# Two attention blocks and two Fourier blocks on one core: 384 and 128 column blocks share a PSUM bank, and one layer norm gets another gate

## The chip, the cores and the metric

The kernel runs on one core of a Trainium2 chip. A core has TensorE (PE, matrix products, with its weight loads as PEld), VectorE (DVE), ScalarE (ACT), GpSimd (POOL) and SyncE (SP, which here issues every DMA), each with its own instruction queue worked in order. They share SBUF, and TensorE writes to eight PSUM banks of 128 partitions x 512 fp32 columns. The metric is the device time of one execution in microseconds (us), the median of several runs.

## The reference

A sequence x of 2048 rows by 512 columns goes through four blocks, A, B, A, B, each with a layer norm in front and a residual around it:

```
x = x + A(layernorm(x)); x = x + B(layernorm(x)); and both again

A: 32 heads of width 16, four segments of 512 rows, for each segment s:
   p     = softmax(q k^T / 4 + causal mask);  a_dot = p v
   a_mem = phi(q) M / (phi(q) z + 1e-6)       phi(t) = t+1 if t > 0 else exp(t)
   o     = g a_mem + (1 - g) a_dot            g = sigmoid(beta) per head
   M += phi(k)^T v;  z += sum phi(k)
   result o @ wo
B: real part of a DFT over rows and columns:  Cr (x Dr^T) - Ci (x Di^T)
```

The mask is causal in the segment, so of the 4 x 4 blocks of 128 x 128 of each head only ten count. The DFT matrices are inputs.

## The kernel before

Products are made from fp16 halves: a value is scaled and split into a high and a low half, and three matmuls (high x high, high x low, low x high) stand for one. Two blocks A+B make a "layer", two layers in all. A layer has four segments (q counts them 0 to 7 over both layers), a segment four *groups* of eight heads (i counts 32 groups). A group's heads are four pairs p = 0..3 of two heads a = 0, 1, which use partitions 0 to 63 and 64 to 127; their matmuls of 64 rows run side by side on TensorE ("64-row mode").

The path of one group:

- `s_ln` (line 550) loads the four 128-row tiles of x of a segment, one after the other, into slots called `xi`; each starts a layer-norm task `t_ln` (line 528: statistics on DVE, power on POOL, scaling on DVE, halves on ACT and POOL, a DMA transpose into `xt`, printed as `g`). A gate ahead of the loop says when a segment's layer norm may start.
- `s_p` (707) projects q and k, `t_split` (609) sends them through DRAM into `qst` and `kst`. `s_v` (732) projects the values into `vt`; for group 3 and later it is gated on the values of the group three before being used.
- `s_x` (802), the *maximum steps*: 64-row matmuls of a query tile t against keys 0 to 128(t+1), and `t_max` (791), one masked maximum on DVE for each head and tile. The maxima are transposed on TensorE and, as `mhl`, written by DMA into the last rows of `qst`, so that the next product subtracts them.
- `s_st` (852), the *score steps*: key tile t against queries from 128t on, 512 - 128t columns. `t_sel` (841) takes the exponential on ACT into an SBUF tile `pt` and zeroes the upper triangle with a select on POOL.
- `s_av` (874): values times scores, fp32, in 32-column mode, accumulated over t into one bank for each a. It waits for all four p of a t, and closes the `pt` tiles of that t.
- `t_merge`, `s_m` (573, 895): denominators through DRAM (`den`, `dc`, `rec`), reciprocal, gating with the memory. `s_o` (930) multiplies with wo, and its result passes through a layer norm into block B (`s_ab`, `s_f`).

A maximum or score step takes two banks (kind `ss`, at most six), one for each a. Blocks of one t share a bank as far as they fit: t of 128, 256, 384 and 512 columns give four, two, one and one block in a bank, so 1 + 2 + 4 + 4 = 11 steps, and a bank with a 384-column block has 128 columns unused. A group has 22 banks of scores, so 22 exponentials and 22 selects. `pt` tiles are SBUF slots with a reserve of 8 and a limit of 12 at a time.

What sets the order of the instructions: the streams above are generators that say what they need next (an engine, operands, slots). A planner (`Plan`, line 45, and the loop at 1126) keeps modelled times of every engine, slot and operand, and emits, step by step, whatever is ready first by its model; ties go to the order of the streams. A `gate` holds a stream until other streams have *emitted* the steps named; it is not a wait on the chip. Nothing is reordered later: each engine runs its instructions in the order in which they were emitted, SP's DMAs too. The planner makes score and maximum steps wait a little for two pairs of banks, so that two steps run in one visit to 64-row mode, and counts 95 ns for a change of mode.

Done-marks that matter here: `("V", i)` the values of group i were projected, `("E", i)` the values of group i were multiplied with the scores (emitted), `("X", i)` the maxima were sent off. `s_wo` (449) loads wo after `("X", 1)` and the hidden DFT matrices (`wd`) after all q and k weights were split; all of block B and the output product wait for its end ("WO").

All instructions pass one helper, so the profile gives line 249 for each; they are told apart by their tiles: `junk` is the masked maximum, `b<-kst,qst` the maximum matmuls, `b<-qst,kst` the score matmuls, `b<-w,vt` the values times scores, `b<-w,g` the value projection and `b<-g,w` the q and k projections of a segment, `w<-b,fac` of ACT the exponentials (with 24 others of 512 columns).

Of the kernel before, what the change touches and what calls it, by code (L numbers as in the profile page):

```python
# [12 lines left out]
AF = mybir.ActivationFunctionType  # L13
# [6 lines left out]
TT = L // 128  # L20
NT = S // 128
NG = 4
HG = H // NG
NP = HG // 2
# [231 lines left out]
def body(ctx: ExitStack, tc: tile.TileContext, x, wq, wk, wv, wo, beta, wd, cs, out):  # L256
    nc = tc.nc
    pl = Plan()
    V, G, A, T, Y = (Eng(e, k, pl) for e, k in zip(
        (nc.vector, nc.gpsimd, nc.scalar, nc.tensor, nc.sync), "VGATY"))  # L260
# [13 lines left out]
    def ps(kind, dt=F32, shape=(128, 512)):  # L274
        return pl.take(kind, shape, dt)

    sb = ps
# [38 lines left out]
    m0, m1, rp, ra = (const.tile([128, 1], F32, name=n) for n in ("m0", "m1", "rp", "ra"))  # L316
    done = set()
    ywritten = set()
    xts, xbs, ots, o2s, phs, avs, pts, drs = {}, {}, {}, {}, {}, {}, {}, {}
    tasks = []  # L320

    def rg(tag, bufs, dt, shape=(128, 512)):
        return work.tile(list(shape), dt, name=tag, bufs=bufs)

    def need(eng, *reads, tag=(), mode="m"):
        return eng, reads, (tag,) if isinstance(tag, str) else tag, mode
# [5 lines left out]
    def gate(*keys):  # L332
        return lambda: all(k in done for k in keys)
# [3 lines left out]
    def spawn(g, to=tasks):  # L337
        to.append([next(g, None), g])
# [15 lines left out]
    f_q, f_k, f_s, f_k2 = ([fac[:, NG * i + g:NG * i + g + 1] for g in range(NG)] for i in range(4))  # L354
# [195 lines left out]
    def s_ln():  # L550
        for q in range(LAYERS * NSEG):
            layer, s = divmod(q, NSEG)
            if q:
                yield gate(("V", q * NG - 1))
            if q > 1:
                yield gate(("O", q - 2))
            xt = None
            for t in range(TT):
                if layer:
                    yield gate(("y", layer - 1, TT * s + t))  # L560
                if q == 0:
                    xi = xi0[t]
                else:
                    yield need("Y", tag="xi")
                    xi = sb("xi")
                    Y.dma_start(xi, srcs[layer][TT * s + t])
                if xt is None:
                    yield need("V", tag="xt")
                    xt = xts[q] = sb("xt", F16, (128, 2, KT, 512))
                yield need("V", xi)  # L570
                spawn(t_ln(xi, xi, xt[:, :, :, 128 * t:128 * t + 128], ("L", q, t)))
# [216 lines left out]
                    pl.close(mu)  # L788
            done.add(("U", i))

    def t_max(sp, mx, a, p0, w, t, left):
        n = 128 * (t + 1)
        for p in range(p0, p0 + w):
            o = (p - p0) * n
            yield need("V", sp)
            junk = rg("junk", 2, BF16)
            V.tensor_tensor_reduce(junk[:, :n], sp[:, o:o + n], cmask[:, 512 - n:], 1.0, -3e38,
                                   OP.add, OP.max, mx[:, a, p, t:t + 1])
        pl.close(sp)
        left[0] -= 1  # L800

    def s_x():
        for i in range(NGRP):
            yield gate(("dq", i), ("dk", i), "CM")
            qs, ks = qst[i % NR], kst[i % NR]
            mx = rg("mx", 2, F32, (128, 2, NP, TT))
            left = [0]
            for t in range(TT):
                n = 128 * (t + 1)
                w = 512 // n  # L810
                for p0 in range(0, NP, w):
                    yield need("T", qs, ks, tag=("ss", "ss"), mode="h")
                    sp = [ps("ss"), ps("ss")]
                    for p in range(p0, p0 + w):
                        o = (p - p0) * n
                        for a in range(2):
                            T.matmul(sp[a][:, o:o + n], qs[64 * a:64 * a + 62, p, 128 * t:128 * t + 128],
                                     ks[64 * a:64 * a + 62, p, 0:n], start=True, stop=True)
                    left[0] += 2
                    for a in range(2):  # L820
                        spawn(t_max(sp[a], mx, a, p0, w, t, left))
            yield lambda: left[0] == 0
            yield need("T", mx, tag="ss")
            pm = ps("ss")
            T.transpose(pm[0:32, 0:128], mx.rearrange("q a p t -> q (a p t)"), identf)
            mhl = rg("mhl", 2, F16, (32, 2, 128))
            yield need("A", pm)
            A.activation(mhl[:, 0], pm[0:32, 0:128], AF.Copy, scale=-2.0 ** -13)
            yield need("V", mhl)
            V.scalar_tensor_tensor(mhl[:, 1], pm[0:32, 0:128], -2.0 ** -13, mhl[:, 0],  # L830
                                   op0=OP.mult, op1=OP.subtract)
            pl.close(pm)
            yield need("Y", mhl)
            for a in range(2):
                for j in range(2):
                    r = 64 * a + 62 + j
                    Y.dma_start(qs[r:r + 1].rearrange("o p (t n) -> o (p t) n", t=TT),
                                mhl[16 * a:16 * a + 16, j, :], est=(610, 500))
            done.add(("X", i))

    def t_sel(sp, pt, w, n, f, keys):
        yield need("A", sp)
        A.activation(pt[:, :w * n], sp[:, :w * n], AF.Exp, scale=f)
        pl.close(sp)
        yield need("G", pt)
        v3 = pt[:, :w * n].rearrange("k (w n) -> k w n", w=w)[:, :, 0:128]
        G.affine_select(v3, v3, pattern=[[0, w], [1, 128]], compare_op=OP.is_ge, fill=0.0,
                        base=0, channel_multiplier=-1)
        for k in keys:
            done.add(k)  # L850

    def s_st():
        for i in range(NGRP):
            yield gate(("X", i))
            qs, ks = qst[i % NR], kst[i % NR]
            for t in range(TT):
                n = 512 - 128 * t
                w = 512 // n
                for p0 in range(0, NP, w):
                    yield need("T", qs, ks, tag=("ss", "ss", "pt", "pt"), mode="h")  # L860
                    sp = [ps("ss"), ps("ss")]
                    for p in range(p0, p0 + w):
                        o = (p - p0) * n
                        for a in range(2):
                            T.matmul(sp[a][:, o:o + n], ks[64 * a:64 * a + 64, p, 128 * t:128 * t + 128],
                                     qs[64 * a:64 * a + 64, p, 128 * t:], start=True, stop=True)
                    for a in range(2):
                        pt = sb("pt")
                        spawn(t_sel(sp[a], pt, w, n, f_s[i % NG], [("pt", i, a, t, p) for p in range(p0, p0 + w)]))
                        for p in range(p0, p0 + w):  # L870
                            pts[i, a, t, p] = (pt, pt[:, (p - p0) * n:(p - p0 + 1) * n])
            done.add(("ST", i))

    def s_av():
        for i in range(NGRP):
            q, g = divmod(i, NG)
            v = vt[i % NR]
            for t in range(TT):
                for a in range(2):
                    yield gate(("v", i), *[("pt", i, a, t, p) for p in range(NP)])  # L880
                    tiles = [pts[i, a, t, p] for p in range(NP)]
                    yield need("T", v, *[x[0] for x in tiles], tag="av" if t == 0 else (), mode="v")
                    if t == 0:
                        avs[i, a] = ps("av")
                    av = avs[i, a]
                    for p in range(NP):
                        T.matmul(av[32 * p:32 * p + 32, 128 * t:],
                                 v[:, t, p].rearrange("k e d -> k (e d)")[:, 16 * a:16 * a + 32], tiles[p][1],
                                 start=(t == 0), stop=(t == TT - 1), skip_group_check=True)
                    for x in {x[0].tensor.name: x[0] for x in tiles}.values():  # L890
                        pl.close(x)
            done.add(("E", i))
            pl.late = q % NSEG == NSEG - 1 and g == NG - 1

# [186 lines left out]
    def s_f():  # L1081
        u = 0
        for layer in range(LAYERS):
            tabs, left = {}, {}
            for j, t in seq[layer]:
# [29 lines left out]
                yield need("T")  # L1115

    streams = [[None, s()] for s in (s_r, s_c, s_st, s_ln, s_w, s_x, s_mem, s_v, s_p, s_ab, s_f, s_wo, s_k)]
    hots += [[None, s()] for s in (s_m, s_o, s_av,)]
    for s in hots + streams:
        s[0] = next(s[1])  # L1120
# [5 lines left out]
    while streams or hots or tasks or lows:  # L1126
# [12 lines left out]
        for s in hots + tasks + streams + lows:  # L1139
            w = s[0]  # L1140
# [11 lines left out]
        if pl.mode != "h":  # L1152
            other = min((r for r, s in ready if s[0][0] == "T" and s[0][3] != "h"), default=1e18)
            for j, (r, s) in enumerate(ready):
                w = s[0]
# [56 lines left out]
```

## Time and profile before

| | |
|---|---|
| median of 3 runs | 1781.19 us (1776.84 to 1781.40) |
| the profiled execution | 1784.39 us, of which the span from first to last instruction is 1782.6 us |
| granted TensorE clock, mean | 0.975 |
| busy in the span | PE 1676.7 us, DVE 1086.1, ACT 911.4, POOL 755.4 |
| matmuls | 11020, of which 2048 in maximum and score steps |
| maxima on DVE | 1024 (256 each of 128, 256, 384 and 512 columns) |
| selects on POOL | 704 |

The page gives busy times, a row of the span in 40 slices, the chain of work that ended last and the costliest groups of instructions, as "out<-in", with count, busy time, mean and the idle time before them. Busy matmuls overlap in the array, so a row's duration is longer than the distance to the next start. The profiled execution is 3.2 us above the median.

### The profile page before, as it was taken

What the parts mean: (1) busy time and instruction counts of PE and PEld (TensorE: products, weight loads), DVE (VectorE), ACT (ScalarE), POOL (GpSimd) and SP (SyncE); (2) the same over time, 40 slices, a digit from 0 to 9 for tenths busy, and PEclk for the clock granted to TensorE, in tenths of its full rate; (3) what the DMA queues carried; (4) which work ended last, traced back from release to release, by engine and by line L of the source; (5) the groups of instructions that cost most, each with busy time, mean ns of one, the idle gap of its engine ahead of it and who ended that gap; (6) DMA issues with size and microseconds to landing.
All of it is one profiled execution on the core that took longest, in us unless ns stands there. A gap on an engine that the chain in (4) does not pass through costs nothing.

```text
span 1782.6 us, 32540 instructions
## 1 busy us (share of the span) xinstructions
PE 1676.7 (94%) x11020; PEld 733.9 (41%) x11020; DVE 1086.1 (61%) x3387; ACT 911.4 (51%) x1585; POOL 755.4 (42%) x1187
## 2 busy tenths in 40 slices
PE   4978799999999999999899998999999999999999
PEld 2424334344444433444444443444444443344444
DVE  7783777477667775545577656754676566342222
ACT  4567666756656758433456764556355535510000
POOL 6354545546544655433335543433553343330000
PEclk9978899999999999999899999999999999999999
DMA  8446536555555533435856745453453542137104
GB/s 214 118 129 155 163 106 142 174 154 154 150 134 158 164 90 116 133 123 171 237 160 195 206 138 131 100 138 110 118 126 107 164 99 71 51 107 254 42 0 136
DMA packets 240983, 242.43 MB, mean 136 GB/s; under 512 B 129776, under 2 KB 152304, under 8 KB 240816
## 3 DMA queue, kind: packets, MB, share of 16 engines
q1 hardware_dynamic: 240816, 240.35, 48.5%
q8 instruction: 87, 1.43, 0.4%
q14 instruction: 80, 0.66, 0.1%
HBM read 152.96 MB, written 63.70 MB: 122 GB/s over the span
## 4 chain that ended last, share of the span: by engine, by line
PE 67%; DMA 11%; DVE 7%; ACT 5%; POOL 4%; issue 4%; SPq 2%; POOLq 0%; ACTq 0%; DVEq 0%
PE b L249 67%; ACT w L249 5%; POOL w L249 3%; DMA w<-w 3%; DVE w L249 2%; SPq L249 2%; DVE junk L249 2%; DMA dc<-den 2%; DMA w<-rec 2%; DMA w<-in_cs_dram 1%; DVE cam L249 1%; DVE bst L249 1%; DMA w<-in_x_dram 1%; DVE y L249 0%; DMA d<-w 0%
## 5 line engine op out<-in xcount | busy, mean ns | idle before, releaser
L249 PE MATMUL b<-w,w 128*128 128x512 f16 x3072 | 714.1, 382 | 12.5 <-ACT w L249 7.1
L249 PEld LDWEIGHTS <-w 128*128 128x128 f16 x4992 | 465.4, 99 | 624.4 <-issue 111.2
L249 POOL TENSOR_TENSOR w<-w,w 128x512 f16<-128x512 f32 (+1 forms) x316 | 379.6, 1208 | 369.1 <-ACT w L249 255.3
L249 ACT ACTIVATE w<-b,fac 128x512 f32<-128x512 f32 (+1 forms) x728 | 420.0, 657 | 205.6 <-PE b L249 196.2
L249 DVE CUSTOM_DVE_ANT_0 junk<-b,cmask 128x128 bf16<-128x128 f32 (+3 forms) x1024 | 441.1, 484 | 105.3 <-PE b L249 104.2
L249 POOL TENSOR_SCALAR_AFFINE_SELECT w<-w 128x128 f32<-128x128 f32 (+2 forms) x704 | 242.8, 356 | 308.6 <-ACT w L249 285.2
L249 DVE SCALAR_TENSOR_TENSOR y<-b,fyu,y 128x512 f32<-128x512 f32 x232 | 173.3, 747 | 220.4 <-PE b L249 219.7
L249 ACT ACTIVATE w<-b 128x512 f16<-128x512 f32 (+1 forms) x240 | 137.9, 597 | 178.7 <-PE b L249 172.3
L249 ACT ACTIVATE w<-w,csc 128x512 f16<-128x512 f32 (+1 forms) x256 | 181.9, 723 | 70.2 <-DVE csc L249 53.6
L249 PE MATMUL b<-g,w 128*128 128x512 f16 x768 | 187.5, 386 | 3.6 <-DMA g<-w 2.8
L249 PE MATMUL b<-wd,w 128*128 128x512 f16 x768 | 181.4, 382 | 0.1
L249 ACT ACTIVATE w<-w 128x512 f16<-128x512 f32 (+1 forms) x144 | 90.5, 631 | 177.9 <-DVE w L249 122.1
L249 PE MATMUL b<-w,vt 128*32 128x512 f32 (+3 forms) x2048 | 177.7, 455 | 1.9 <-POOL w L249 1.7
L249 DVE SCALAR_TENSOR_TENSOR w<-b,w 128x512 f16<-128x512 f32 x128 | 87.8, 687 | 100.4 <-ACT w L249 100.0
L249 PE MATMUL b<-kst,qst 62*128 62x128 f16 (+3 forms) x1024 | 124.7, 305 | 18.1 <-ACT w L249 5.6
L249 PE MATMUL b<-qst,kst 64*128 64x512 f16 (+3 forms) x1024 | 121.1, 304 | 13.3 <-ACT w L249 7.7
L249 PE MATMUL b<-w,g 128*128 128x128 f16 x1536 | 97.4, 221 | 11.9 <-DMA w<-w 6.9
L249 PEld LDWEIGHTS <-g 128*128 128x128 f16 x1536 | 89.7, 99 | 26.9 <-issue 17.7
L249 PEld LDWEIGHTS b<-w,vt 128*32 128x32 f32 x2048 | 56.5, 111 | 96.4 <-issue 51.1
L249 PE MATMUL b<-wo,w 128*128 128x512 f16 x384 | 88.0, 385 | 0.9 <-ACT w L249 0.9
L249 PEld LDWEIGHTS <-kst 64*128 64x128 f16 x1024 | 37.5, 94 | 124.5 <-issue 118.8
L249 DVE TENSOR_REDUCE cam<-w 128x1 f32<-128x512 f32 x128 | 81.0, 675 | 6.8 <-DMA w<-in_cs_dram 6.7
(101 smaller groups left out, 902.8 us busy)
## 6 DMA issues: line engine op xcount, KB each, us to landing
w<-in_cs_dram SPq DMA_DIRECT2D x128, 256.0 KB
cc<-w SPq DMA_DIRECT2D x128, 256.0 KB
w<-cc SPq DMA_DIRECT2D x128, 256.0 KB
w<-w SPq DMA_DIRECT2D x96, 256.0 KB
d<-w SPq DMA_DIRECT2D x128, 128.0 KB
w<-rec SPq DMA_DIRECT2D x56, 256.0 KB
w<-in_x_dram SPq DMA_DIRECT2D x32, 256.0 KB
qst<-d SPq DMA_DIRECT2D x64, 128.0 KB
```

Of the source, the lines that this page charges most:

```text
L249: r = f(*args, **kw)
```

## The change

Three things are changed, and one follows from them.

1. The gate of segment two's layer norm (q = 1): it may start once the first group's values times scores were emitted, `("E", 0)`, instead of after the fourth group's value projection, `("V", 3)`. The other segments' gates stay.
2. Maximum and score steps are built by a new function `steps`. It takes groups of tiles that share a bank. Maxima: two steps of 256-column blocks, four of a 128 and a 384-column block, four of 512 columns. Scores: four steps of 512, two of two 256-column blocks, four of a 384 and a 128-column block (t = 1 and t = 3). Ten steps each instead of eleven; every bank is full.
3. An exponential now always covers 512 columns, and a select covers one 128-column block (t = 0) or two (with their distance taken from the step): 20 of each for a group.
4. As blocks t = 1 and t = 3 lie in the same `pt` tile, values are taken in the order t = 0, 2, 1, 3, and a tile is closed when a count of its blocks (`uses`) reaches zero.

```
-                yield gate(("V", q * NG - 1))
+                yield gate(("E", 0) if q == 1 else ("V", q * NG - 1))
...
+    def steps(widths, *groups):
+        out = []
+        for ts in groups:
+            per = 512 // sum(widths[t] for t in ts)
+            for p0 in range(0, NP, per):
+                o, step = 0, []
+                for p in range(p0, p0 + per):
+                    for t in ts:
+                        step.append((p, t, o, widths[t]))
+                        o += widths[t]
+                out.append(step)
+        return out
+
+    def t_max(sp, mx, a, step, left):
+        for p, t, o, n in step:
...
+            for step in steps([128 * (t + 1) for t in range(TT)], (1,), (0, 2), (3,)):
+                yield need("T", qs, ks, tag=("ss", "ss"), mode="h")
+                sp = [ps("ss"), ps("ss")]
+                for p, t, o, n in step:
                     for a in range(2):
-                        spawn(t_max(sp[a], mx, a, p0, w, t, left))
+                        T.matmul(sp[a][:, o:o + n], qs[64 * a:64 * a + 62, p, 128 * t:128 * t + 128],
+                                 ks[64 * a:64 * a + 62, p, 0:n], start=True, stop=True)
...
-    def t_sel(sp, pt, w, n, f, keys):
+    def t_sel(sp, pt, step, f, keys):
         yield need("A", sp)
-        A.activation(pt[:, :w * n], sp[:, :w * n], AF.Exp, scale=f)
+        A.activation(pt, sp, AF.Exp, scale=f)
         pl.close(sp)
         yield need("G", pt)
-        v3 = pt[:, :w * n].rearrange("k (w n) -> k w n", w=w)[:, :, 0:128]
+        w = len(step)
+        v3 = pt.rearrange("k (c n) -> k c n", n=128)[:, 0:4 if w > 1 else 1:step[-1][2] // 128 if w > 1 else 1, :]
...
+            for step in steps([512 - 128 * t for t in range(TT)], (0,), (2,), (1, 3)):
+                yield need("T", qs, ks, tag=("ss", "ss", "pt", "pt"), mode="h")
...
+                    spawn(t_sel(sp[a], pt, step, f_s[i % NG], [("pt", i, a, t, p) for p, t, _, _ in step]))
+                    uses[pt.tensor.name] = len(step)
...
     def s_av():
...
-            for t in range(TT):
+            for t in (0, 2, 1, 3):
...
-                                 start=(t == 0), stop=(t == TT - 1), skip_group_check=True)
-                    for x in {x[0].tensor.name: x[0] for x in tiles}.values():
-                        pl.close(x)
+                                 start=(t == 0), stop=(t == 3), skip_group_check=True)
+                    for x, _ in tiles:
+                        uses[x.tensor.name] -= 1
+                        if not uses[x.tensor.name]:
+                            pl.close(x)
```

More of the change, by code (lines that the diff above doesn't have):

```diff
@@ L318, in body @@
     ywritten = set()
+    uses = {}
     xts, xbs, ots, o2s, phs, avs, pts, drs = {}, {}, {}, {}, {}, {}, {}, {}
@@ L789, in s_mem @@
             done.add(("U", i))
[L791 to L794, printed above, removed]
+    def steps(widths, *groups):
[12 more added lines that the diff above has]
+        for p, t, o, n in step:
             yield need("V", sp)
@@ L807, in s_x @@
             left = [0]
-            for t in range(TT):
[L809 to L819, printed above, removed]
-                    for a in range(2):
-                        spawn(t_max(sp[a], mx, a, p0, w, t, left))
+            for step in steps([128 * (t + 1) for t in range(TT)], (1,), (0, 2), (3,)):
+                yield need("T", qs, ks, tag=("ss", "ss"), mode="h")
+                sp = [ps("ss"), ps("ss")]
+                for p, t, o, n in step:
+                    for a in range(2):
+                        T.matmul(sp[a][:, o:o + n], qs[64 * a:64 * a + 62, p, 128 * t:128 * t + 128],
+                                 ks[64 * a:64 * a + 62, p, 0:n], start=True, stop=True)
+                left[0] += 2
+                for a in range(2):
+                    spawn(t_max(sp[a], mx, a, step, left))
             yield lambda: left[0] == 0
@@ L855, in s_st @@
             qs, ks = qst[i % NR], kst[i % NR]
[L856 to L866, printed above, removed]
-                    for a in range(2):
[L868 to L871, printed above, removed]
+            for step in steps([512 - 128 * t for t in range(TT)], (0,), (2,), (1, 3)):
+                yield need("T", qs, ks, tag=("ss", "ss", "pt", "pt"), mode="h")
+                sp = [ps("ss"), ps("ss")]
+                for p, t, o, n in step:
+                    for a in range(2):
+                        T.matmul(sp[a][:, o:o + n], ks[64 * a:64 * a + 64, p, 128 * t:128 * t + 128],
+                                 qs[64 * a:64 * a + 64, p, 128 * t:], start=True, stop=True)
+                for a in range(2):
+                    pt = sb("pt")
+                    spawn(t_sel(sp[a], pt, step, f_s[i % NG], [("pt", i, a, t, p) for p, t, _, _ in step]))
+                    uses[pt.tensor.name] = len(step)
+                    for p, t, o, n in step:
+                        pts[i, a, t, p] = (pt, pt[:, o:o + n])
             done.add(("ST", i))
@@ L877, in s_av @@
             v = vt[i % NR]
-            for t in range(TT):
+            for t in (0, 2, 1, 3):
                 for a in range(2):
```

## The prediction

> **What bounds the kernel now.** I read the page first (parts 1, 2 and 4), then the busy time of each engine in stretches, then what TensorE waited for in the early stretches, and last the timeline of TensorE and of the DMA queue around segment two's layer norm.
>
> ```profile
> PE 1676.7 (94%) x11020; PEld 733.9 (41%) x11020; DVE 1086.1 (61%) x3387; ACT 911.4 (51%) x1585; POOL 755.4 (42%) x1187
> PE 67%; DMA 11%; DVE 7%; ACT 5%; POOL 4%; issue 4%; SPq 2%; POOLq 0%; ACTq 0%; DVEq 0%
> ```
> ```profile
> 85.00:137.00 52.00, 40.41 (x320) 15.12 (x317) 43.87 (x172) 33.42 (x61) 24.64 (x54) 0.80 0.46 136
> 137.00:202.00 65.00, 50.29 (x392) 25.38 (x394) 33.46 (x110) 46.94 (x82) 34.95 (x46) 0.85 0.65 147
> 240.00:860.00 620.00, 596.28 (x3846) 257.55 (x3845) 402.96 (x1196) 374.86 (x640) 316.46 (x455) 0.99 0.50 143
> 860.00:1420.00 560.00, 537.03 (x3872) 238.16 (x3870) 361.03 (x1232) 312.17 (x551) 244.02 (x407) 0.99 0.54 145
> ```
>
> TensorE bounds it: 94% of the span and two thirds of the chain. But not everywhere. The columns of the stretches are length, then busy time of PE, PEld, DVE, ACT and POOL, the granted clock, the DMA share and GB/s. From 240 to 1420 us TensorE is busy 96% at a clock of 0.99: there a change is worth what it takes off TensorE's own time. Between 85 and 202 us it idles 11.6 + 14.7 = 26.3 us, and runs at a clock of 0.80 and 0.85: there latency counts. That is the end of segment one and the start of segment two, where the second edit acts.
>
> ```profile
> PE b L249 <- DVE mx L249: 8.5, 8, 4.6
> PE b L249 <- ACT w L249: 6.6, 11, 4.1
> PE b L249 <- DVE mx L249: 6.4, 1, 6.4
> ```
>
> The first row is from the waits between 85 and 137 us, the other two from those between 137 and 225 us (total, times, longest). The long stalls are waits for a group's maxima and for the exponentials, not for the layer norm by name. Segment two's first projection starts at 137.21:
>
> ```profile
> 84.44 0.43 PE L249 MATMUL b<-w,vt 128*32 128x128 f32 x8 [0.16 <-POOL w L249]
> 85.59 2.17 PE L249 MATMUL b<-w,g 128*128 128x128 f16 x36
> 137.21 3.41 PE L249 MATMUL b<-g,w 128*128 128x512 f16 x15 [0.58 <-DMA w<-w]
> ```
>
> **The change, part one: the gate.** The first row above ends the first group's values (what the new gate waits for), at 84.9; the second is the main part, 36 of 48 matmuls, of the fourth group's value projection (the old gate), up to 87.8. On TensorE they lie 2.9 us apart. What matters is the DMA queue, which works in program order:
>
> ```profile
> 85.33 1.23 SPq L249 DMA_DIRECT2D den<-w  x2
> 86.66 3.21 SPq L249 DMA_DIRECT2D qst<-mhl  x4
> 89.92 0.59 SPq L249 DMA_DIRECT2D y<-in_wo_dram  x1
> 90.56 0.50 SPq L249 DMA_DIRECT2D y<-in_wd_dram  x1
> 91.64 0.65 SPq L249 DMA_DIRECT2D w<-in_x_dram  x1
> 102.19 0.43 SPq L249 DMA_DIRECT2D w<-in_x_dram  x1
> 112.90 0.41 SPq L249 DMA_DIRECT2D w<-in_x_dram  x1
> 119.58 0.40 SPq L249 DMA_DIRECT2D w<-in_x_dram  x1
> 127.39 5.74 SPq L249 DMA_TRANSPOSE g<-w  x2
> ```
> ```profile
> 102.84 0.68 DVE L249 BATCH_NORM_STATS2 bst<-w 128x6 f32<-128x512 f32 x1
> 121.90 0.69 DVE L249 BATCH_NORM_STATS2 bst<-w 128x6 f32<-128x512 f32 x1
> ```
>
> The four loads of x for segment two are issued one at a time: the loop emits the next load only when the planner takes the one before as landed. The first is issued at 91.64, behind the loads of wo and wd (3 MB), and its statistics start 11.2 us later; the fourth, with nothing large ahead of it, needs 121.90 - 119.58 = 2.3 us. With the new gate the first load stands about where the den pair stands now (85.33; that pair also follows the first group's values), ahead of wo and wd, and should land by about 88. The second then goes out around 89 to 92 and takes the place behind wo and wd that the first has now. So the row of loads moves up by one place: the fourth goes out at 112.90 instead of 119.58, 6.7 us earlier, and the projection could start at about 130.5.
>
> The ends: two loads may slip in ahead, and the fourth goes out where the second does now, 119.58 - 102.19 = 17.4 us earlier. On the other side, each transpose that moves forward sits on the DMA queue ahead of other groups' transfers. The pair at 127.39 held the queue for 5.7 us; if such a pair stands ahead of a group's maxima (qst<-mhl), its exponentials start up to 5.7 us later: +5.7. I take -5, nearer the one-place shift than either end: little of the idle lies between 130.5 and 137, but everything behind the projection moves up with it, and the remaining stalls (4.1 and 6.4 us, on exponentials and maxima) keep some back. The layer norm's work itself is only moved: four tiles of DVE, POOL and ACT work and four transposes run 7 us sooner, DVE being busy 43.87 of 52 us in that stretch.
>
> **Part two: the steps.** Before, a group has 11 maximum steps and 11 score steps, each filling a pair of banks; the 384-column ones leave a quarter of each bank empty. After, the 128-column blocks fill those quarters: 10 and 10. Matmuls (2048 in all) and maxima (1024) stay as they are in number and width, so DVE gains nothing. What goes are two exponentials and two selects a group.
>
> ```profile
> L249 ACT ACTIVATE w<-b,fac 128x512 f32<-128x512 f32 x472 | 290.8, 694 | 137.3 <-PE b L249 128.3 <-issue 7.0 <-POOL w L249 1.0
> L249 ACT ACTIVATE w<-b,fac 128x384 f32<-128x384 f32 x256 | 130.7, 587 | 68.3 <-PE b L249 67.9
> 91.79 6.73 ACT L249 ACTIVATE w<-b,fac 128x512 f32<-128x512 f32 x12 [3.39 <-PE b L249]
> ```
>
> ACT: 22 exponentials over 10,240 columns become 20 over the same columns. By the means, 128 columns cost 694 - 587 = 107 ns, so the part without columns is 694 - 428 = 266 ns; back to back, twelve took 6.73 us or 561 ns each, which leaves about 130. So 64 x 0.13 to 0.27 = 8 to 17 us of ACT, which is busy 51%: nothing where TensorE is full, at most two shorter waits a group where it is not. Of POOL I say the same (64 selects fewer, 42% busy).
>
> TensorE: a step interrupts the 128-row matmuls with a pair of 64-row ones, and going in and out costs something:
>
> ```profile
> 245.10 3.41 PE L249 MATMUL b<-w,w 128*128 128x512 f16 x15
> 248.44 0.39 PE L249 MATMUL b<-qst,kst 64*128 64x512 f16 x2
> 248.77 1.47 PE L249 MATMUL b<-w,w 128*128 128x512 f16 x6
> 250.17 0.61 PE L249 MATMUL b<-qst,kst 64*128 64x512 f16 x4
> 250.71 1.47 PE L249 MATMUL b<-w,w 128*128 128x512 f16 x6
> ```
>
> Start to start, 15 wide matmuls take 3.34 us and 6 (from 248.77) take 1.40: 0.216 us each and 0.10 on leaving. One pair takes 0.33, two 0.54: 0.21 a pair and 0.12 on leaving. A visit costs 0.22 us beside its columns. In the timeline of the whole span I count 444 unbroken stretches of such matmuls (231 for maxima, 213 for scores), the first and the last of them these:
>
> ```profile
> 42.50 0.67 PE L249 MATMUL b<-kst,qst 62*128 62x128 f16 x12
> 1553.43 0.40 PE L249 MATMUL b<-qst,kst 64*128 64x128 f16 x8
> ```
>
> for 32 x 22 = 704 steps, 0.63 a step. The 64 steps that go save 64 x 0.63 = 40 visits, 40 x 0.22 = 8.9 us. Ends: every step that goes was a visit of its own, 64 x 0.22 = 14.1; none was (steps regroup), 0. I take 9, by the count.
>
> The order of the value matmuls becomes 0, 2, 1, 3, because blocks 1 and 3 now come out of the same banks. Before, only block 3 had to follow the last step; now block 1 does too.
>
> ```profile
> 174.04 1.50 PE L249 MATMUL b<-w,vt 128*32 128x384 f32 x16
> 184.47 0.64 PE L249 MATMUL b<-w,vt 128*32 128x128 f32 x16
> ```
>
> So the tail after a group's last step grows from 0.64 to 2.1 us. Where TensorE has other work (from 240 us on) that costs nothing; in the eight groups of the first two segments at most 8 x 1.5 = 12 us. There is still other work in most of them: I take 2.
>
> Sum: -5 - 9 + 2 = -12 us against the profiled execution's 1784.39, or 1772; that execution is 3.2 us above the median of the runs, so 1769.
>
> **A rule of the Trainium skill** bears on the stalls. These are the stretches (clock in the third column from the right) in and behind the 4.6 us stall for maxima, and a group row that the rivals need:
>
> ```profile
> 110.00:115.00 5.00, 1.81 (x19) 1.12 (x20) 4.93 (x16) 1.46 (x4) 0.56 (x1) 0.59 0.27 66
> 115.00:120.00 5.00, 3.13 (x7) 0.59 (x6) 5.00 (x35) 1.89 (x3) 1.44 (x2) 0.50 0.33 65
> 120.00:125.00 5.00, 4.60 (x20) 0.94 (x18) 4.93 (x16) 4.68 (x9) 3.38 (x8) 0.50 0.36 107
> 125.00:130.00 5.00, 4.01 (x25) 0.79 (x21) 4.70 (x13) 4.51 (x10) 4.60 (x11) 0.70 0.27 52
> ```
> ```profile
> L249 DVE TENSOR_SCALAR w<-w,mv,rs 128x512 f32<-128x512 f32 x56 | 39.0, 696 | 14.4 <-POOL rs L249 14.2
> ```
>
> The clock falls to half and is still at 0.70 in the last row, 10 us or more after the stall; at these clocks the busy time holds 1.81 x 0.41 + 3.13 x 0.50 + 4.60 x 0.50 + 4.01 x 0.30 = 5.8 us of lost time. "TensorE: Matmul & The Clock Gate", section "What's actually happening", says that the clock goes to half after an idle window of about 3.4 us and comes back after as long a busy one. The drop agrees with these rows; the slow return does not.
>
> **The rivals.**
> *One stall and its slow clock go.* The 4.6 us stall waits for maxima, with DVE at 4.93 of 5 us. The two long DVE operations of the first layer-norm tile (0.68 from its row at 102.84 and 0.70 from the row above) move ahead, so the stall may shrink by 1.4 to 3.2 us. If the clock then holds, 1.4 + 5.8 = 7 us more are gained: 1762. By the same page's threshold that is what would happen. Against it: the second and third tiles move into the place of the first.
>
> *Slower: the score tiles run out.* An exponential's tile holds two blocks for the last four steps, and is freed only when both were used. At most 12 tiles may be out. Before, six (blocks 2 and 3) were held at a group's end; now eight. The next group's first eight then wait for values, and TensorE stalls for exponentials as it does once today (4.1 us, above). Each such stall costs 4.1; three cancel the gain, and five, in segments one and two where nothing covers them, give 1769 + 20.5 = 1789. For it: that stall exists today, and the clock falls behind such stalls. Against it: score steps of two groups rarely adjoin.
>
> *No difference.* The planner re-orders everything for the new steps; fewer steps regroup into as many visits (0 instead of -9) and the projections of segment two, earlier by 7 us, run into the same stalls (0 instead of -5), with the tail at +2: 1783, within 0.3%.
>
> **How the numbers follow.** Chances: forecast 0.46, the clock's rival 0.16, no difference 0.14, slower 0.24. A measurement of this kernel tells about 0.3%, 5.3 us, from no change. Forecast and clock rival are faster: 0.62; same 0.14; slower 0.24. The forecast's own range is 1760 to 1777. The whole range reaches down to both lower ends together (-17 - 14 = -31, 1750) and up past the slower case, 1792.
>
> **What would show it.** The first load of segment two ahead of wo, and the fourth near 113; its first projection near 130; 640 exponentials of 512 columns and none of 384; 640 selects; about 400 visits; TensorE's idle from 240 us on not above the 46.7 us of today (23.7 + 23.0). It is wrong if waits for exponentials or for score tiles grow, or if the loads stay behind wo and wd.

## The result and the profile after

The changed kernel takes 1769.33 us (median of 7 runs, 1764.51 to 1774.31), the kernel before, run beside it, 1781.4 us: a ratio of 0.9924, 95% interval 0.9904 to 0.9943. (The medians lie 12.1 us apart; the ratio, which is used from here on, makes it 13.5.) The profiled execution took 1769.47 us with a span of 1767.7. From the page after, span and busy times; then the stretches used in the prediction (length, busy time and instructions of PE, PEld, DVE, ACT, POOL, clock, DMA share, GB/s):

```profile
span 1767.7 us, 32331 instructions
PE 1669.0 (94%) x11020; PEld 746.7 (42%) x11020; DVE 1090.7 (62%) x3392; ACT 898.9 (51%) x1521; POOL 740.5 (42%) x1118
```
```profile
85.00:240.00 155.00, 129.44 (x957) 57.82 (x950) 109.86 (x407) 105.68 (x182) 80.35 (x134) 0.86 0.52 142
240.00:860.00 620.00, 598.31 (x3864) 264.53 (x3862) 411.42 (x1187) 372.50 (x619) 312.37 (x429) 0.99 0.51 146
860.00:1420.00 560.00, 539.29 (x3909) 243.86 (x3909) 366.63 (x1248) 308.92 (x532) 249.43 (x398) 0.99 0.55 144
```

and the first of these stretches in the kernel before:

```profile
85.00:240.00 155.00, 126.52 (x912) 53.80 (x910) 107.05 (x383) 101.85 (x180) 79.09 (x134) 0.83 0.56 147
```

TensorE still bounds the kernel. To tell work from waiting I add up, over stretches of 5 us, TensorE's busy time times the granted clock, and call the sum its *own time*: what its work would take at full clock. The rest of the span is idle time and time lost to a low clock. It is known for one profiled execution of each kernel.

| | span | own time | idle | lost to the clock |
|---|---|---|---|---|
| before | 1782.6 | 1645.1 | 105.9 | 31.6 |
| after | 1767.7 | 1639.1 | 98.7 | 29.9 |
| difference | -14.9 | -6.0 | -7.2 | -1.7 |

Idle and clock loss together fell by 3.4 us between 85 and 240 us, by 4.1 between 240 and 860, by 3.5 between 860 and 1420, and rose by 2.1 before 85 us. The gain is spread over the span; less than a quarter of it lies where the gate acts.

What the new gate does there is stronger than forecast. From the DMA queue, and from TensorE with the first projection of segment two (`b<-g,w`), after (rows between are left out):

```profile
82.89 1.37 SPq L249 DMA_DIRECT2D w<-in_x_dram  x3
86.80 1.23 SPq L249 DMA_DIRECT2D den<-w  x2
89.64 0.67 SPq L249 DMA_DIRECT2D w<-in_x_dram  x1
94.72 0.59 SPq L249 DMA_DIRECT2D y<-in_wo_dram  x1
95.36 0.50 SPq L249 DMA_DIRECT2D y<-in_wd_dram  x1
96.50 9.43 SPq L249 DMA_TRANSPOSE g<-w  x2
```
```profile
113.71 0.82 PE L249 MATMUL b<-g,w 128*128 128x512 f16 x3
190.50 2.84 PE L249 MATMUL b<-w,g 128*128 128x128 f16 x48
197.72 0.36 PE L249 MATMUL b<-cam,ones 128*128 128x4 f32 x2 [4.37 <-DVE cam L249]
210.65 5.35 PE L249 MATMUL b<-wo,w 128*128 128x512 f16 x24
```

All four loads pass ahead of wo and wd, and the projection starts at 113.7 instead of 137.2, 23.5 us earlier. The lead dwindles on the way. The last split of the hidden DFT matrix on POOL, which block B waits for, ends at 192.6 instead of 204.8, 12 us earlier (after, then before):

```profile
191.39 1.16 POOL L249 TENSOR_TENSOR wd<-y,wd 128x512 f16<-128x512 f32 x1 [0.20 <-ACT y L249]
```
```profile
203.60 1.15 POOL L249 TENSOR_TENSOR wd<-y,wd 128x512 f16<-128x512 f32 x1
```

TensorE then waits 4.4 us for the first scale of the sequence DFT (`cam`); the first product with wo comes at 210.65, 8 us *later* than before; and the first product with `wd`, the start of block B, at 222.75 instead of 224.13, 1.4 us earlier (before, then after):

```profile
202.46 7.32 PE L249 MATMUL b<-wo,w 128*128 128x512 f16 x24
224.13 2.72 PE L249 MATMUL b<-wd,w 128*128 128x512 f16 x6
```
```profile
222.75 2.77 PE L249 MATMUL b<-wd,w 128*128 128x512 f16 x6
```

The waits between 137 and 240 us, after, and the selects:

```profile
PE b L249 <- DVE mx L249: 5.8, 10, 1.4
PE b L249 <- ACT w L249: 5.8, 16, 1.4
PE b L249 <- DVE cam L249: 4.4, 1, 4.4
```
```profile
L249 POOL TENSOR_SCALAR_AFFINE_SELECT w<-w 128x256 f32<-128x256 f32 x384 | 153.9, 414 | 103.5 <-ACT w L249 96.4 <-DMA kst<-d 2.2 <-DMA den<-w 2.0
L249 POOL TENSOR_SCALAR_AFFINE_SELECT w<-w 128x128 f32<-128x128 f32 x256 | 75.6, 306 | 151.8 <-ACT w L249 148.7 <-issue 1.6 <-PE b L249 0.5
```

The single stalls of 4.1 and 6.4 us are gone; many short ones and one new long one stand in their place. The selects are 640 and the exponentials all 512 wide, as foreseen.

### The profile page after: what moved, and what is told of

It reads as the page before. It is cut to its first block, busy times and chain, and to the rows that moved or that the text cites. A ratio compares the mean times of both kernels' runs of the same rounds, so it can differ in the third digit from the quotient of the medians.

```text
span 1767.7 us, 32331 instructions
## 1 busy us (share of the span) xinstructions
PE 1669.0 (94%) x11020; PEld 746.7 (42%) x11020; DVE 1090.7 (62%) x3392; ACT 898.9 (51%) x1521; POOL 740.5 (42%) x1118
## 5 line engine op out<-in xcount | busy, mean ns | idle before, releaser
L249 DVE CUSTOM_DVE_ANT_0 junk<-b,cmask 128x256 bf16<-128x256 f32 (+3 forms) x1024 | 437.1, 483 | 66.0 <-PE b L249 65.4
L249 ACT ACTIVATE w<-b,fac 128x512 f32<-128x512 f32 x664 | 407.4, 696 | 128.7 <-PE b L249 125.8
L249 POOL TENSOR_SCALAR_AFFINE_SELECT w<-w 128x256 f32<-128x256 f32 (+1 forms) x640 | 229.5, 371 | 255.3 <-ACT w L249 245.1
L249 PE MATMUL b<-w,vt 128*32 128x512 f32 (+3 forms) x2048 | 174.1, 455 | 0.8 <-ACT w L249 0.5
L249 PE MATMUL b<-kst,qst 62*128 62x256 f16 (+3 forms) x1024 | 121.1, 306 | 19.3 <-DVE mx L249 9.1
L249 PEld LDWEIGHTS b<-w,vt 128*32 128x32 f32 x2048 | 60.2, 111 | 91.3 <-issue 58.9
```

The source lines that it names most:

```text
L249: r = f(*args, **kw)
```

## The experiments

Theory: the gate acts where it stands, by an earlier projection, and the steps by fewer changes of TensorE's mode; the two add up. Rivals: one of them is the whole gain; or the planner's new order of everything behind is worth as much as either. Ratios are to runs of the kernel before on the same chip.

### The parts alone

Gate only (`e1`):

```
-                yield gate(("V", q * NG - 1))
+                yield gate(("E", 0) if q == 1 else ("V", q * NG - 1))
```

> The kernel before with the new gate alone. Prediction's terms: -5 us (1776), anything from -17 to +6 within its ends. Rival 'the gate is the whole gain': -12 us (1769), with segment two's first projection near 114 as in the changed kernel. Rival 're-ordering': the first projection moves up by 20 us and more, and the time stays within 5 us, because the output product (first wo matmul, 202.5 us before) does not come earlier.

Measured 1.0012 (0.9994 to 1.0029): no change. The projection starts at 136.66, half a microsecond earlier. Only one of the four loads got ahead of wo and wd:

```profile
86.33 0.42 SPq L249 DMA_DIRECT2D w<-in_x_dram  x1
91.79 0.59 SPq L249 DMA_DIRECT2D y<-in_wo_dram  x1
93.52 0.63 SPq L249 DMA_DIRECT2D w<-in_x_dram  x1
104.12 0.42 SPq L249 DMA_DIRECT2D w<-in_x_dram  x1
115.21 0.41 SPq L249 DMA_DIRECT2D w<-in_x_dram  x1
```

This is the picture the prediction drew, one load ahead and three behind, and it is worth nothing here. The fourth load goes out at 115.21 instead of 119.58, 4.4 us earlier, but the last transpose still goes out at 129.81 (the pair before: 127.39): the lead is lost between the load and the projection.

Steps only (`e2`): the changed kernel with the old gate.

> The changed kernel with the old gate. Prediction's terms: -9 + 2 = -7 us (1774), with about 400 stretches of 64-row matmuls against 444. Rival 'the steps are the whole gain': -12 us. Rival 'the gate is the whole gain': within 3 us of the kernel before.

Measured 1.0064 (1.0047 to 1.0082): *slower*. Own time is 1642.0, 3 us below the kernel before, but idle and clock loss rose from 137.5 to 148.5. The loss is in the second layer:

```profile
85.00:240.00 155.00, 130.35 (x961) 56.83 (x954) 110.28 (x399) 106.46 (x184) 82.98 (x132) 0.87 0.53 145
240.00:860.00 620.00, 593.01 (x3817) 259.81 (x3814) 406.86 (x1180) 366.92 (x609) 309.90 (x429) 0.99 0.51 143
860.00:1420.00 560.00, 529.59 (x3786) 234.96 (x3785) 357.95 (x1226) 304.66 (x522) 235.35 (x378) 0.97 0.54 140
```

With the old gate TensorE is even busier between 85 and 240 us than in the changed kernel (130.35 against 129.44); between 860 and 1420, where the two kernels have the same code, it is 10 us less busy and at a lower clock. The work of the two is the same, as a gate adds none, and so are TensorE's 11020 matmuls. What differs is the planner's order, and three operations that it put on GpSimd instead of VectorE (1121 and 1118 instructions on GpSimd); with that, the time differs by 1.4%.

Maximum steps only (`e3`) and score steps only (`e4`), each in the kernel before, the score steps with their order of values:

```
 e3:
+            for step in steps([128 * (t + 1) for t in range(TT)], (1,), (0, 2), (3,)):
 e4:
+            for step in steps([512 - 128 * t for t in range(TT)], (0,), (2,), (1, 3)):
...
+            for t in (0, 2, 1, 3):
```

> The kernel before with the new maximum steps alone; exponentials, selects, value order and gate as before. By visits: half of the saved ones, -4 to -6 us. If DVE's maxima set the pace there, no gain (within 3 us), as DVE's instructions are the same in number and width.

> The kernel before with the new score steps and the new order of values alone. By visits: -4 to -6 us, less 2 for the longer tail. If the saved exponentials count, more: ACT is 8 to 17 us less busy, and the difference to the maximum steps alone is what that is worth.

Maximum steps: 1.0057 (1.0037 to 1.0077), own time 1649.4. Score steps: 0.9976 (0.9961 to 0.9992), own time 1639.0. Taken singly, in one order each and against the order of the kernel before, only the score steps lower TensorE's own time, and only they bring time.

So the parts are +0.12%, +0.57% and -0.24%, and together -0.76%. They do not add. That left the planner's order.

### One order, one thing moved

The planner's steps (8727, the same set with either gate) were recorded and played back instead of chosen by modelled times; only the 29 steps of segment two's layer norm were moved, each to stand after as many other steps as in the other kernel.

```
-            first = min(r for r, _ in ready)
-            best = next(q for q in ready if q[0] <= first + SLACK)
+            best = min(ready, key=lambda q: place_of(q[1]))
```

> The instructions of the changed kernel in its own recorded order, with only segment two's layer norm (29 of 8727 planner steps) put back to where the old gate has it; the rest keeps its order, and what waits for the layer norm follows as soon as it may. If the gate acts where it stands (theory of the prediction): about 1774, 5 us over the changed kernel, at most 17 over. If the gate's effect is that the planner orders everything behind it anew: 1769 to 1774. If the gate is worth the 24 us by which steps alone and steps with gate differ: about 1793.

> The reverse: the order of the steps-alone kernel (1793), with only segment two's layer norm moved forward to where the new gate has it. Gate acting where it stands: about 1788. Re-ordering: 1788 to 1793, with the 18 us that the second layer's start lost still lost. Gate worth 24 us: about 1769.

The changed kernel's order with the layer norm put back: 0.9993 (0.9977 to 1.0008), against 0.9924, 12 us worse. The steps-only order with the layer norm moved forward: 1.0106 (1.0079 to 1.0134), against 1.0064, 7 us worse. Both moves lose, in opposite directions. In the first, between 85 and 240 us, TensorE is 12 us less busy than in the changed kernel, with one stall of 8 us ahead of the projection, which now starts at 132.71:

```profile
85.00:240.00 155.00, 117.14 (x831) 52.44 (x830) 101.59 (x373) 98.94 (x170) 77.05 (x125) 0.80 0.51 141
```
```profile
132.71 9.36 PE L253 MATMUL b<-g,w 128*128 128x512 f16 x36 [8.00 <-DMA w<-w]
```

In the second, all loads are issued by 91.00, and yet the projection stands where the recorded order had it and starts at 142.13, 6 us later than without the move, while three transposes hold the DMA queue for 11 us ahead of the first group's `rec`:

```profile
92.27 10.96 SPq L253 DMA_TRANSPOSE g<-w  x3
105.81 0.34 SPq L253 DMA_DIRECT2D rec<-dc  x1
107.51 1.24 SPq L253 DMA_TRANSPOSE g<-w  x1
```

So each order fits the layer norm it was planned with, and neither run gives the gate a price of its own: the 12 us hold only for an order that counted on the early layer norm.

### The same work in other orders

One constant of the planner's model, the price of a change of mode, set to 100 and to 90 ns (no work is added or removed):

```
-HOLD, SWITCH = 700.0, 95.0
+HOLD, SWITCH = 700.0, 100.0
```

> The kernel before with one constant of the planner's model changed (a change of TensorE's mode counted as 100 ns instead of 95); no work is added or removed. If the planner's order is worth several us by itself: anywhere from 1770 to 1795, more than 4 us from the kernel before. If orders are alike: within 4 us of it.

> The changed kernel with the same constant changed. If the change's gain is that of its steps and gate: within 4 us of 1769. If it is partly the luck of one order: anywhere from 1765 to 1795, on the average higher than 1769.

> The kernel before with the planner's price of a change of mode at 90 ns: one more order of the same work. 1775 to 1795; TensorE's own time 1645 to 1655.

> The changed kernel with the price at 90 ns: one more order of its work. TensorE's own time about 1639. If the change is worth 6 to 9 us by its work and the rest is order: 1770 to 1785, below the run with the same constant in the kernel before. If 1769 is typical of it: 1766 to 1772.

| price of a change of mode | before: ratio, own time | changed: ratio, own time | projection, changed |
|---|---|---|---|
| 95 ns (as given) | 1 , 1645.1 | 0.9924 (0.9904 to 0.9943), 1639.1 | 113.7 |
| 100 ns | 1.0003 (0.9987 to 1.0020), 1654.6 | 0.9979 (0.9963 to 0.9994), 1638.5 | 113.3 |
| 90 ns | 1.0026 (1.0011 to 1.0041), 1650.3 | 0.9990 (0.9974 to 1.0006), 1637.6 | 137.7 |

In each pair the changed kernel is the faster one, by 0.76, 0.24 and 0.36%: 8 us on the average, 4 to 14 singly. The order alone moves the changed kernel by 0.66%, 12 us, and the one as given is the best of the three. (With the order, the planner also puts up to seven operations on VectorE instead of GpSimd or the other way.) Steps only (1.0064) is one more order of the same work; against the kernel before at the same price it is a loss. So the gain in time depends on which orders are counted. An early projection (113.3 us) goes with 0.9979, a late one (137.7 us) with 0.9990: these do not show that it brings time. In the first, block B starts at 229.68 us, 5.8 us later than in the kernel before at the same price (223.83), though the projection is 25 us earlier.

How many loads of x pass ahead of wo and wd is the planner's choice too. With the new gate it is four in the changed kernel, three at 100 ns, and none at 90 ns, where the first goes out at 87.72, behind wo at 86.54. Maximum steps only, with the old gate, has one ahead (86.42 against 89.48).

### Score steps with the gate

> New score steps and value order with the new gate, maxima as before. TensorE's own time (busy, brought to full clock) near 1639 as with both new steps, since the score steps alone had it. If the maximum steps bring nothing and the gate acts where it stands: 1768 to 1772, as fast as the changed kernel. If the order decides: anywhere from 1765 to 1790.

Measured 0.9977 (0.9960 to 0.9995), the same as the score steps without the gate (0.9976); the projection starts at 135.18 against 135.29. Own time 1638.5. The new gate moved no load here: all four stay behind wo and wd (the first at 89.54, wo at 88.37), so this run does not price an early layer norm. It does not beat the changed kernel, which stays the fastest of all that were run.

### What a visit costs

In the changed kernel, the wait for two pairs of banks taken out:

```
-TWICE, EARLY, BESIDE = 1000.0, 0.0, 1000.0
+TWICE, EARLY, BESIDE = 0.0, 0.0, 1000.0
```

> The changed kernel with the planner's wait for two pairs of banks taken out, so that steps go one by one: by the emitted order 408 visits to 64-row mode instead of 361. At 0.22 us a visit TensorE's own time (busy, at full clock) rises by 47 x 0.22 = 10 us, from 1639 to about 1649. If a visit costs nothing: 1637 to 1642. The time itself moves with the order too.

Measured 1.0021 (1.0005 to 1.0038). On TensorE the visits (unbroken stretches of maximum and score matmuls) rose from 361 to 408, 47 as expected, and own time from 1639.1 to 1643.7: 4.6 us, 0.10 a visit and half of what was expected. Every unbroken stretch of one mode (wide, 64-row, 32-column), counted in the order of the matmuls' starts, over all fourteen kernels:

```
kernel               stretches   own time
score alone / +gate  904 / 904 1639.0 / 1638.5
changed kernel          851    1639.1
  with 100 / 90 ns   872 / 871 1638.5 / 1637.6
  layer norm late       842    1637.7
steps only              885    1642.0
  layer norm early      885    1640.0
no pairing              945    1643.7
before                  947    1645.1
  with 100 / 90 ns   963 / 960 1654.6 / 1650.3
gate only               943    1645.9
maxima only             961    1649.4
```

All nine kernels with the new score steps have less own time than any of the five with the old ones. A line through all fourteen has a slope of 0.11 us a stretch, with 2.8 us of scatter, near the 0.10 and 0.12 that the rows of the kernel before gave for leaving a mode. But it mainly joins these two groups. Within the nine the slope is 0.05, and no pairing, with 94 stretches more than the changed kernel, pays 4.6 us, 0.05 each. So the price of a change of mode is not settled, and fewer changes are shown as the cause only in part.

Where the own time was saved can be read by charging each matmul the time until the next one starts (its own end, if TensorE idles then), times the clock. From the kernel before to the changed one, the values times scores fall from 162.9 to 159.1 us, the wide fp16 products (projections, wo and block B) from 1206.3 to 1204.1, and the maxima and scores stay (203.6 and 204.0). Averaged over the five kernels with the old and the nine with the new score steps, own time falls by 9.4 us: 3.6 in the values, 3.6 in the wide products, 2.1 in maxima and scores. So over a third lies in the values, which come in 122 stretches before and 105 after. That fits the values of blocks 1 and 3 now coming together; the order of values was not run alone.

## Why the prediction was right, and where it was not

*The total.* Forecast -12 us and 1769; measured -12.1 and 1769.3. The sign held, and the mechanism of the steps in part; the exact hit did not come from right terms and is luck. By the three pairs of orders the change is worth about 8 us on the average, and one more order of the same work (steps only) is slower than the kernel before.

*Steps: -9 by 40 visits of 0.22 us.* Own time fell 6.0 us in this pair, and 11.6 on the average of three orders (1650.0 to 1638.4): the term was of the right size (6.0, 16.1 and 12.7 in the three). Its 444 stretches counted a passage from maxima to scores as a new visit; the visits proper are 399, or 0.57 a step, and 361 after: 38 fewer where 40 were counted on. The place was in part another: in this pair 3.8 of the 6.0 us lie in the values times scores, where the prediction saw only a cost, and a visit taken back cost 0.10 us, not 0.22. Of the two steps, only the score steps showed a gain when made alone.

*Order of values: +2.* Not seen apart, as no run has it alone. TensorE's idle time just before the values fell from 1.9 to 0.8 us over the span, and their busy time fell too, by the groups of the two pages (before, then after); a cost of the longer tail was not seen, but waits behind the values are not in these rows.

```profile
L249 PE MATMUL b<-w,vt 128*32 128x512 f32 (+3 forms) x2048 | 177.7, 455 | 1.9 <-POOL w L249 1.7
```
```profile
L249 PE MATMUL b<-w,vt 128*32 128x512 f32 (+3 forms) x2048 | 174.1, 455 | 0.8 <-ACT w L249 0.5
```

*Gate: -5, by a row of loads moved up one place.* The step that failed is "the row of loads moves up by one place", and with it the price. In the changed kernel three loads go out together, the fourth 29.9 us earlier than before (89.64), and the projection starts 23.5 us earlier, not 6.7; with the gate alone one load goes ahead and the projection moves 0.5 us; in two other kernels with the new gate no load goes ahead. The gate permits; the planner decides. What part of a shift is kept was put at 5 of 6.7; in the stretch from 85 to 240 us 3.4 us were kept of 23.5, and block B starts 1.4 us earlier. The prediction named stalls on maxima and exponentials as what keeps gain back; it did not follow the lead as far as the output product and block B's preparation, before which both kernels idle (6.4 us up to 201 us before, 4.4 us up to 198 after). Why the product with wo comes later was not tried. With planner and kernel free, the gate brought +0.1% on the kernel before, nothing on the score steps, where it moved no load, and -1.4% on both steps, most of that (17.7 us of idle and clock loss) in the second layer. Its own price stays open; it can't be had while the order behind it changes too.

*The clock's rival* (the 4.6 us stall goes, 7 us more gained). The stall went, and the clock between 105 and 130 us rose from 0.66 to 0.97; both stretches, before and after:

```profile
105.00:130.00 25.00, 16.90 (x104) 4.67 (x103) 24.56 (x90) 14.15 (x27) 13.97 (x26) 0.66 0.32 76
```
```profile
105.00:130.00 25.00, 22.54 (x191) 9.70 (x186) 20.13 (x68) 15.04 (x28) 8.82 (x17) 0.97 0.61 159
```

But over 85 to 240 us the loss to the clock is 16.9 us against 17.4: it came back elsewhere, at 95 to 105 and at 165 to 185 us. After:

```profile
165.00:170.00 5.00, 2.71 (x10) 0.62 (x10) 5.00 (x27) 2.31 (x4) 1.79 (x2) 0.80 0.49 108
170.00:175.00 5.00, 3.88 (x8) 0.71 (x8) 4.61 (x22) 3.81 (x8) 5.00 (x5) 0.50 0.35 105
175.00:180.00 5.00, 4.20 (x18) 1.72 (x20) 0.99 (x1) 5.00 (x10) 4.43 (x11) 0.50 0.00 2
```

The waits between 160 and 180 us are short ones behind each step, the longest 1.1 us, mostly for maxima on a full DVE:

```profile
PE b L249 <- DVE mx L249: 3.0, 6, 1.1
PE b L249 <- ACT w L249: 0.8, 2, 0.6
```

The Trainium skill, in "TensorE: Matmul & The Clock Gate", section "A second HAM failure mode: psum-queue depth-cycling", describes a kernel whose frequent short idles between groups of matmuls make the clock swing between half and full. These rows agree with that, and not with the rule of one long window by which the rival was priced.

*The slower rival* (score tiles run out). Waits of TensorE for ACT fell from 26.1 to 19.7 us over the span, none longer than 2.4; before and after:

```profile
PE b L249 <- ACT w L249: 26.1, 36, 4.1
```
```profile
PE b L249 <- ACT w L249: 19.7, 43, 2.4
```

A slower outcome was near all the same, by another way: both steps with the old gate were 0.64% slower, through stalls of the second layer that no row of the kernel before could show. *No difference* named the re-ordering rightly, but as something that takes back 14 us at most; it moves the same work by 12 us between three orders, and by 24 us between the two gates.

## What to carry to other kernels

Where a planner writes out the order, one measurement of an edit measures the edit and one order; run the same edit under a few harmless settings of the planner before giving the edit a price. Split TensorE's span into busy time at full clock, idle and clock loss: the first answered to the order by 1.5 us where the time moved by 12 (three orders of the changed kernel), though by 9.5 us in the kernel before, so it too wants several orders. It showed that the new score steps lower TensorE's own time, which single times did not. Follow a lead to the place where the bound engine is full again before pricing it: 23.5 us at the projection were 1.4 at the start of block B.

## What had not been expected

- Over a third of the own time that was saved lies in the values times scores, which the prediction held for a cost.
- A clock of 0.50 (170 to 180 us) came without any idle time above 1.1 us in it or in the 10 us before it. TensorE idled 2.3 of 5 us in the row before (165 to 170), in several pieces.
- The order alone, with the same work, was worth 0.66% in the changed kernel and 0.26% in the kernel before; counting the old gate, which adds no work, 1.4% in the changed kernel.
